# Attention block: row maxima split on GpSimd, turned by VectorE and carried through DRAM; row-sum copy in two parts; output weights rounded on GpSimd

## The chip, the cores and the metric

One core of one Trainium2 chip. Five engines run their own instruction queues: TensorE (PE, with its weight loads PEld), VectorE (DVE), ScalarE (ACT), GpSimd (POOL) and SyncE (SP), which issues most DMAs. The metric is the device time of one execution in microseconds (us), as the median of several runs.

## The reference

One transformer block on 2048 tokens of width 640, in float32:

```python
qkv = layernorm(x) @ wqkv                     # 32 heads of 20
scores = einsum("bhqd,bhkd->bhqk", q, k) * 20 ** -0.5
h = x + reshape(einsum("bhqk,bhkd->bhqd", softmax(scores), v)) @ wo
out = h + (silu(z @ w_gate) * (z @ w_up)) @ w_down   # z = layernorm(h), F = 1728
```

## The kernel before, in words

Three stages follow one another. First come layernorm and the qkv projection, whose results go to DRAM. Then the attention, from about 323 to 1475 us of the span. Then the output projection and the feed-forward part.

**Units and steps.** The attention is cut into 32 units `u`: eight groups of four heads, times four chunks of 512 queries (`u % 4` is the chunk). A unit has 16 steps `kt`, one for each 128 keys. A step multiplies four heads' keys with the queries (`scores`, L1187: four matmuls, each into one of four PSUM banks that are used in turn, `ps_one`), ACT takes the exponential out of each bank (L1193, 128x512), and two steps later PE multiplies the values with the exponentials (`weigh`, L1197: eight matmul records, into the bank `acc`). These eight open each step in PE's order (`W` in the strings `ORDER`); in this text **W** is their start, and the distance from one W to the next is the length of a step.

**Row maxima.** The exponent needs each query's largest score beforehand. Its negative is carried as two extra rows of the query tile `q_stk` (a rounded high part and the rest), against rows of ones in the keys, so that the score matmul subtracts it (62 rows: 60 and these 2). The maxima of later units are computed in the steps of earlier ones: each step has three more matmuls into `ps_max` (three banks in turn, L244), and DVE reduces each to one column of `mx` (L250). A list `singles` hands them out in order; a unit's maxima end some steps before the unit starts: about 5 steps for `u % 4 == 3` and for unit 1, at least 10 for the rest.

**The end of a unit's maxima.** When its last one is out, `max_all` (L257) reduces `mx` on DVE to `neg`, 128 queries x 16. Two steps later, at the step's W, `max_finish` turns it: PE transposes it (L264) into one of the four `ps_one` banks, ACT rounds it out of the bank (L88, 16x128), DVE subtracts for the rest (L89), and SP issues four DMAs (L271) into the two rows of `q_stk`.

**Row sums.** After a unit's last step `row_sums` (L1207) copies `acc` to the tile `o` on ACT. The next unit's weighing goes to the same bank, so its first W waits for that copy. DMAs gather the row sums, DVE takes their reciprocals after step 4 (L1218), a DMA spreads them (`rb`), GpSimd multiplies at step 9 (L1232), and SP stores `o` at step 11 (L1235).

**GpSimd and SP beside it.** From unit 1 on each step but 3 and 4 also takes one task of `prepare_weights`: GpSimd splits feed-forward weights into high and low parts (L1005, L1006), which SP stores to DRAM one task later (L996). `split_wo` (L883) splits the five row blocks of `wo` in units 25 to 27, at steps 2 and 3: ACT rounds (L88), GpSimd subtracts (L89). Each engine works through its own queue in the order of the program text; an instruction that waits holds all that stand behind it on that engine.

Of the kernel before, what the change touches and what calls it, by code (L numbers as in the profile page):

```python
# [9 lines left out]
F32 = mybir.dt.float32  # L10
BF16 = mybir.dt.bfloat16
F32R = mybir.dt.float32r
I32 = mybir.dt.int32
AF = mybir.ActivationFunctionType
ALU = mybir.AluOpType
AX = mybir.AxisListType

P = 128
# [7 lines left out]
CH = 512  # L26
NC = S // CH
TPC = CH // P
NF = (F + P - 1) // P
G = 4  # L30
# [3 lines left out]
NPART = 3 * DH  # L34
ROW = P // 2
# [9 lines left out]
def tile_block(ctx: ExitStack, tc: tile.TileContext, x, wqkv, wo, wg, wu, wd, out):  # L45
    nc = tc.nc
    x = x[0]
    out = out[0]
# [7 lines left out]
    v_d = dram.tile([S, NG, VG], F32, name="v_d")  # L56
    o_d = dram.tile([D, S], F32, name="o_d")
    r_d = dram.tile([H, S], F32, name="r_d")
    z_d = [dram.tile([P, 2 * ND * CH], F32R, name=f"z_d{c}") for c in range(2)]
    t_d = [dram.tile([P, 8 * CH], F32R, name=f"t_d{i}") for i in range(2)]  # L60
    w_d = [dram.tile([P, 8, 4 * P], F32R, name=f"w_d{f}") for f in range(NF)]
# [25 lines left out]
    def split(src, hi, lo, lo_engine=nc.vector):  # L87
        nc.scalar.activation(hi, src, AF.Copy)  # L88
        lo_engine.tensor_tensor(out=lo, in0=src, in1=hi.bitcast(F32), op=ALU.subtract)  # L89
# [46 lines left out]
    keys, queries, values = {}, {}, {}  # L136
# [117 lines left out]
    def max_all(u):  # L254

        ends[u] = stk.tile([P, G * TPC], F32, name="neg", tag="neg", bufs=2)
        nc.vector.tensor_reduce(  # L257
            ends[u], mxs[u].rearrange("p b h t k -> p (b h t) k"), axis=AX.X, op=ALU.max, negate=True
        )

    def max_finish(u):

        m = (ps_one if u else ps_max)()[: G * TPC, :P]
        nc.tensor.transpose(m, ends.pop(u), ident)  # L264
        parts = stk.tile([G * TPC, 2, P], F32R, name="m2", tag="m2", bufs=1)
        split(m, parts[:, 0], parts[:, 1], nc.vector)
        for b in range(2):
            for i in range(2):
                row = b * ROW + NPART + i
                first = b * 2 * TPC  # L270
                nc.sync.dma_start(  # L271
                    queries[u][row : row + 1].bitcast(F32).rearrange(
                        "r j (t p) -> r (j t) p", t=TPC
                    ),
                    parts[first : first + 2 * TPC, i, :].bitcast(F32),
                )
# [604 lines left out]
        nc.sync.dma_start(wo_raw[k], wo[k * P : (k + 1) * P, :])  # L881

    def split_wo(k):  # L883
        split(wo_raw.pop(k), wo_hi[:, k, :], wo_lo[:, k, :], nc.gpsimd)

    def projection(c, ps_of):

# [315 lines left out]
            )  # L1203

    def row_sums(acc, *queues):
        o = pc.tile([P, CH], F32, name="o", bufs=1)
        nc.scalar.activation(o, acc, AF.Copy)  # L1207
        r = pc.tile([P, 16], F32, name="r")
        for j in range(G):
            queues[j % len(queues)].dma_start(  # L1210
                r[32 * j : 32 * j + 32, :],
                o[32 * j + DH : 32 * j + DH + 1, :].rearrange("r (p f) -> r p f", p=32),
            )
        return o, r
# [21 lines left out]
                o_d[h * DH : (h + 1) * DH, c * CH : (c + 1) * CH], o[32 * j : 32 * j + DH, :]  # L1236
            )

    todo, tail, accs, closing, now = [], [], {}, {}, [0]
    singles = [[(*a, b) for a in rest] for b in range(2)]  # L1240
    left = {u: sum(2 for a in rest if a[0] == u) for u in range(1, NU)}

    def next_max(b):
        if singles[b]:
            a = singles[b].pop(0)
            max_one(*a)
            left[a[0]] -= 1
            if left[a[0]] == 0:
                max_all(a[0])
                closing[a[0]] = now[0] + 2  # L1250

    def weigh_next():
        u, kt, probs = todo.pop(0)
# [9 lines left out]
    for u in range(NU):  # L1263
        g, c = divmod(u, NC)
        if g == NG - 1 and c >= 2:
            _, first, ln, flips, _ = ahead
            extra = [*first, *ln, lambda: None, *flips]
        for kt in range(NT):
            now[0] = u * NT + kt
            ready = [v for v, at in closing.items() if at == now[0]]  # L1270
            probs = [pp.tile([P, 2, CH], F32, name="probs") for _ in range(2)]
            heads = [[0, 2], [1, 3]]
            order = ORDER[now[0] % 2] if singles[0] or singles[1] else "sSsSW"
            for op in order:
                if op in "mM":
                    next_max(int(op == "M"))
                elif op in "sS":
                    scores(u, kt, heads[op == "S"].pop(0), probs)
                else:
                    if len(todo) == 2:  # L1280
                        weigh_next()
                    for v in ready:
                        max_finish(v)
                    if extra:
                        extra.pop(0)()
                    if preparing and u and kt not in (3, 4):
                        preparing.pop(0)()
                    if now[0] == (NU - NC) * NT + 8:
                        unit_ring, last_ring = weight_rings()
                        unit_ring.fill()  # L1290
                        last_ring.fill()
            todo.append((u, kt, probs))
            if kt == 6 and u + 3 < NU:
                load_queries(u + 3)
            if kt == 10 and u == 0:
                fill_ones(k_stk[1])
            if kt >= 8 and kt % 2 == 0 and c == 1 and g + 1 < NG:
                load_keys(g + 1, slice((kt - 8) // 2 * CH, (kt - 6) // 2 * CH))
            if kt >= 8 and kt % 2 == 0 and c == 2 and g + 1 < NG:
                load_values(g + 1, (kt - 8) // 2 * TPC, (kt - 6) // 2 * TPC)  # L1300

            sooner = u >= NU - 2
            if kt == (3 if sooner else 4) and tail:
                reciprocals(u - 1, tail[0][2], nc.sync)
                rb = spread(u - 1, nc.sync)
            if kt == (6 if sooner else 9) and tail:
                store_o(u - 1, tail[0][1], rb, nc.gpsimd, None)
            if kt == (7 if sooner else 11) and tail:
                store_o(u - 1, tail.pop()[1], rb, None, nc.sync)
            if g == NG - 1 and c >= 1:  # L1310
                at = 8 if sooner else NT - 4
                if kt == at:
                    ahead = projection(
                        c - 1, ps_max if c < NC - 1 else (lambda: ps_b())
                    )
                if kt in (at, at + 1, 12 if sooner else 14):
                    ahead[0][min(kt - at, 2)]()
                    if kt == at + 1 and c < NC - 1:
                        ahead[4]()
            k = 2 * (u - NU + 8)  # L1320
            if kt in (12, 13) and 0 <= k + kt - 12 < ND:
                if k + kt == 12:
                    assert not preparing
                    wo_hi = pc.tile([P, ND, D], F32R, name="wo_hi", bufs=1)
                    wo_lo = pc.tile([P, ND, D], F32R, name="wo_lo", bufs=1)
                load_wo(k + kt - 12)
            if kt in (2, 3) and 0 <= k + kt - 4 < ND:
                split_wo(k + kt - 4)
# [566 lines left out]
```

## Time and profile before

| what | value |
|---|---|
| median of three runs | 2043.51 us (2040.27 to 2043.73) |
| profiled execution, its own time | 2038.82 us |
| its span, first to last instruction | 2037.0 us |
| mean granted TensorE clock | 0.999 |
| span of the attention stage with row maxima | about 323 to 1400 us |
| HBM traffic over the span | 151 GB/s |

A group row names the line, engine, operation, output and inputs, shape and count, then the busy time in us and the mean of one in ns, then the idle time of the engine before these instructions and who ended it. A row of the timeline has the start in us, the length in us, engine, line, operation, tiles, shape and how many instructions were merged into it; in brackets stands the idle time before it and what ended it. A row of stages has the stretch, its length, and each engine's busy time.

### The profile page before, as it was taken

What the parts mean: (1) busy time and instruction counts of PE and PEld (TensorE: products, weight loads), DVE (VectorE), ACT (ScalarE), POOL (GpSimd) and SP (SyncE); (2) the same over time, 40 slices, a digit from 0 to 9 for tenths busy, and PEclk for the clock granted to TensorE, in tenths of its full rate; (3) what the DMA queues carried; (4) which work ended last, traced back from release to release, by engine and by line L of the source; (5) the groups of instructions that cost most, each with busy time, mean ns of one, the idle gap of its engine ahead of it and who ended that gap; (6) DMA issues with size and microseconds to landing.
All of it is one profiled execution on the core that took longest, in us unless ns stands there. A gap on an engine that the chain in (4) does not pass through costs nothing.

```text
span 2037.0 us, 40049 instructions
## 1 busy us (share of the span) xinstructions
PE 2012.7 (99%) x14322; PEld 1249.9 (61%) x14322; DVE 1607.9 (79%) x2826; ACT 1445.2 (71%) x2855; POOL 774.1 (38%) x1103
## 2 busy tenths in 40 slices
PE   8999999999999999999999999999999999999999
PEld 6989995343334333334333433345598888888888
DVE  5677778888888888888888888886378666676677
ACT  4677778999999999999999999987633222211221
POOL 6464423334342444352400011011146454754555
PEclk9999999999999999999999999999999999999999
DMA  7877563452634534435512131311158654974542
GB/s 244 255 244 260 175 206 89 116 161 79 187 104 124 166 115 143 149 127 176 156 46 79 27 94 44 92 62 55 33 184 302 220 192 157 344 273 158 202 150 94
DMA packets 194062, 310.01 MB, mean 152 GB/s; under 512 B 47760, under 2 KB 82576, under 8 KB 192840
## 3 DMA queue, kind: packets, MB, share of 16 engines
q1 hardware_dynamic: 187272, 283.85, 43.0%
q0 software_dynamic: 6496, 23.60, 4.0%
q8 instruction: 114, 1.87, 0.4%
q14 instruction: 84, 0.69, 0.1%
q10 hardware_dynamic: 96, 0.00, 0.0%
HBM read 207.75 MB, written 98.83 MB: 151 GB/s over the span
## 4 chain that ended last, share of the span: by engine, by line
PE 87%; DMA 3%; DVE 1%; issue 1%; POOL 1%; ACT 1%; SPq 1%; ACTq 0%; DVEq 0%; POOLq 0%
PE acc L1197 24%; PE ps_one L1187 16%; PE ps_a L1358 15%; PE ps_max L244 12%; PE ps_b L1452 8%; PE ps_one L568 6%; PE ps_max L211 2%; PE ps_max L918 2%; PE ps_b L918 1%; DMA units<-w_d 1%; DMA halves<-j_d 0%; DMA h<-in_A_x 0%; PE ps_max L953 0%; DVE tmp L1573 0%; ACT o L1207 0%
## 5 line engine op out<-in xcount | busy, mean ns | idle before, releaser
L1193 ACT ACTIVATE probs<-ps_one 128x512 f32<-128x512 f32 x2048 | 1056.7, 614 | 62.3 <-PE ps_one L1187 37.6
L250 DVE TENSOR_REDUCE mx<-ps_max 128x1 f32<-128x512 f32 x1472 | 926.2, 684 | 106.9 <-PE ps_one L1187 75.6
L1187 PE MATMUL ps_one<-q_stk,k_stk 62*128 62x512 f32 x2048 | 586.0, 450 | 2.8 <-DVE m L89 1.8
L1197 PE MATMUL acc<-probs,v_stk 128*32 128x512 f32 x4096 | 545.2, 604 | 0.0
L1187 PEld LDWEIGHTS ps_one<-q_stk,k_stk 62*128 62x128 f32 x2048 | 251.5, 184 | 432.7 <-ACT probs L1193 398.3
L244 PE MATMUL ps_max<-k_stk,q_stk 60*128 60x512 f32 x1472 | 381.2, 425 | 0.0
L244 PEld LDWEIGHTS ps_max<-k_stk,q_stk 60*128 60x128 f32 x1472 | 271.6, 186 | 24.1 <-DVE mx L250 0.9
L1573 DVE TENSOR_TENSOR tmp<-ps_a,tmp 128x512 f32<-128x512 f32 x208 | 141.2, 689 | 120.3 <-PE ps_a L1358 94.6
L233 DVE TENSOR_REDUCE mx<-ps_max 128x2 f32<-128x512 f32 x288 | 180.6, 685 | 66.5 <-PE ps_max L211 63.4
L1232 POOL TENSOR_TENSOR o<-o,rb 128x512 f32<-128x512 f32 x31 | 39.9, 1287 | 413.3 <-DMA q_stk<-q_d 241.5
L1197 PEld LDWEIGHTS acc<-probs,v_stk 128*32 128x32 f32 x4096 | 80.6, 108 | 174.8 <-issue 166.2
L223 ACT ACTIVATE ps_max<-ps_max 128x512 f32<-128x512 f32 x288 | 151.7, 583 | 47.5 <-PE ps_max L211 44.7
L1452 PE MATMUL ps_b<-halves,yp 128*128 128x320 f32 x1032 | 179.3, 308 | 2.0 <-DMA halves<-j_d 1.2
L1452 PEld LDWEIGHTS ps_b<-halves,yp 128*128 128x128 f32 x1032 | 165.1, 188 | 18.6 <-POOL yp L89 1.5
L1358 PE MATMUL ps_a<-t,units 128*128 128x512 f32 x624 | 162.6, 396 | 0.0
L1358 PE MATMUL ps_a<-z,units 128*128 128x512 f32 x516 | 133.9, 394 | 0.0
L89 POOL TENSOR_TENSOR yp<-y,yp 128x256 fp32r<-128x256 f32 x96 | 60.4, 629 | 188.2 <-ACT yp L88 188.2
L1358 PEld LDWEIGHTS ps_a<-t,units 128*128 128x128 f32 x624 | 112.6, 188 | 18.9 <-ACT tmp L1586 0.3
L1457 DVE TENSOR_TENSOR h<-ps_b,h 128x320 f32<-128x320 f32 x248 | 110.0, 481 | 6.9 <-PE ps_b L1452 5.4
L568 PE MATMUL ps_one<-z_hi,w_lo 64*128 64x512 f32 x380 | 113.7, 395 | 0.0
L568 PE MATMUL ps_one<-z_hi,w_hi 64*128 64x512 f32 x380 | 113.1, 396 | 0.0
L568 PE MATMUL ps_one<-z_lo,w_hi 64*128 64x512 f32 x380 | 111.7, 393 | 0.0
(211 smaller groups left out, 2643.3 us busy)
## 6 DMA issues: line engine op xcount, KB each, us to landing
units<-w_d SPq DMA_DIRECT2D x186, 256.0 KB
w_d<-stage SPq DMA_DIRECT2D x106, 256.0 KB
halves<-j_d SPq DMA_DIRECT2D x70, 320.0 KB
j_d<-stage SPq DMA_DIRECT2D x42, 320.0 KB
k_stk<-k_d SPq DMA_DIRECT2D x64, 160.0 KB
q_stk<-q_d SPq DMA_DIRECT2D x64, 160.0 KB
raw<-k_d SPq DMA_DIRECT2D x62, 160.0 KB
raw<-q_d SPq DMA_DIRECT2D x54, 160.0 KB
```

Source lines behind the costliest of these rows:

```text
L223: nc.scalar.activation(ps, ps, AF.Relu)
L233: nc.vector.tensor_reduce(mx[:, b, :, t, kc], ps.rearrange("p (j n) -> p j n", j=2), axis=AX.X, op=ALU.max,)
L244: nc.tensor.matmul(ps, queries[u][rows, pair, t * P : (t + 1) * P], keys[u // NC][rows, pair, kc * CH : (kc + 1) * CH], start=True, stop=True,
L250: nc.vector.tensor_reduce(mxs[u][:, b, pair, t, kc : kc + 1], ps, axis=AX.X, op=ALU.max)
L568: nc.tensor.matmul(ps, a[rows], b[rows], start=(i == n == 0), stop=(i == 1 and n == last), skip_group_check=True,)
L1187: nc.tensor.matmul(ps, keys[u // NC][rows, p, kt * P : (kt + 1) * P], queries[u][rows, p, :], start=True, stop=True,)
L1193: nc.scalar.activation(probs[p][:, b, :], ps, AF.Exp, scale=scale)
L1197: nc.tensor.matmul(acc[32 * j : 32 * j + 32, :], values[u // NC][:, kt, j * VW : j * VW + 32], probs[j // 2][:, j % 2, :], start=(kt == 0) ...
L1358: nc.tensor.matmul(ps.rearrange("p (t n) -> p t n", t=TPC), w[k][:, i], z[k][:, :, j], start=(first and m == 0), stop=(last and m == len(n ...
L1452: nc.tensor.matmul(ps, a, b, start=(n == 0), stop=(n == len(pairs) - 1))
L1457: nc.vector.tensor_tensor(out=h, in0=ps, in1=h, op=ALU.add)
L1573: add = lambda out, ps, x: nc.vector.tensor_tensor(out=out, in0=ps, in1=x, op=ALU.add)
```

## The change

1. **Which units.** Units with `u % 4 == 3` and unit 1 keep `max_finish`. The other 22 (2, 4, 5, 6, 8, 9, 10, ... 28, 29, 30) go another way, in three pieces.
2. **`max_parts`** at the end of the step: GpSimd rounds `neg` and subtracts for the rest, both into one tile of 128x32.
3. **`max_turn`** four steps later: DVE turns that tile in blocks of 32x32, and SP writes it to DRAM (`m_d`, two tensors in turn).
4. **`max_load`** six steps after the end: SP loads it in four DMAs of 32 pieces of 128 bytes into the two rows of `q_stk`.
5. `max_all` is issued after all of the step's maxima, not right behind the unit's last one. `later` replaces `closing`.
6. **Row sums:** ACT copies 384 of `acc`'s 512 columns, DVE the other 128; `o` has two buffers.
7. **`split_wo`:** GpSimd does the rounding too.

```diff
-        split(wo_raw.pop(k), wo_hi[:, k, :], wo_lo[:, k, :], nc.gpsimd)
+        raw = wo_raw.pop(k)
+        nc.gpsimd.tensor_copy(wo_hi[:, k, :], raw)
+        nc.gpsimd.tensor_tensor(
+            out=wo_lo[:, k, :], in0=raw, in1=wo_hi[:, k, :].bitcast(F32), op=ALU.subtract
+        )
...
+    def max_parts(u):
+        neg = ends[u]
+        both = ends[u] = stk.tile([P, 2, G * TPC], F32R, name="neg2", bufs=2)
+        nc.gpsimd.tensor_copy(both[:, 0], neg)
+        nc.gpsimd.tensor_tensor(
+            out=both[:, 1], in0=neg, in1=both[:, 0].bitcast(F32), op=ALU.subtract
+        )
+    def max_turn(u):
+        turned = stk.tile([P, 2 * G * TPC], F32, name="turned", bufs=2)
+        nc.vector.transpose(turned, ends.pop(u).bitcast(F32).rearrange("p i n -> p (i n)"))
+        nc.sync.dma_start(m_d[u % 2], turned)
+    def max_load(u):
+        n = 2 * TPC
+        rows = m_d[u % 2].rearrange("(q i r) c -> i r q c", q=4, i=2)
+        for b in range(2):
+            for i in range(2):
+                row = b * ROW + NPART + i
+                dst = queries[u][row : row + 1].bitcast(F32).rearrange("r j c -> r (j c)")
+                nc.sync.dma_start(dst, rows[i, b * n : (b + 1) * n])
...
     def row_sums(acc, *queues):
-        o = pc.tile([P, CH], F32, name="o", bufs=1)
-        nc.scalar.activation(o, acc, AF.Copy)
+        o = pc.tile([P, CH], F32, name="o", bufs=2)
+        most = 3 * P
+        nc.scalar.activation(o[:, :most], acc[:, :most], AF.Copy)
+        nc.vector.tensor_copy(o[:, most:], acc[:, most:])
...
             if left[a[0]] == 0:
-                max_all(a[0])
-                closing[a[0]] = now[0] + 2
+                full.append(a[0])
...
-                    for v in ready:
-                        max_finish(v)
+                    for f in later.pop(now[0], ()):
+                        f()
...
             todo.append((u, kt, probs))
+            for v in full:
+                max_all(v)
+                if v % NC == NC - 1 or v == 1:
+                    later.setdefault(now[0] + 2, []).append(lambda v=v: max_finish(v))
+                else:
+                    max_parts(v)
+                    later.setdefault(now[0] + 4, []).append(lambda v=v: max_turn(v))
+                    later.setdefault(now[0] + 6, []).append(lambda v=v: max_load(v))
+            full.clear()
```

Three places show the order that results. On PE, at the start of unit 8, where unit 9's maxima are turned, before (`acc` is the weighing, `ps_one` are scores, `ps_max` maxima, `neg` the maxima to turn):

```order
L1197 MATMUL acc<-probs,v_stk_5591 32x512 x4
L264 MATMUL ps_one<-ident,neg 16x128
L1187 MATMUL ps_one<-q_stk,k_stk_123 128x512 x2
L244 MATMUL ps_max<-k_stk_123,q_stk 128x512 x2
L1187 MATMUL ps_one<-q_stk,k_stk_123 128x512 x2
```

and now:

```order
L1227 MATMUL acc<-probs,v_stk_5593 32x512 x4
L1217 MATMUL ps_one<-q_stk,k_stk_125 128x512 x2
L245 MATMUL ps_max<-k_stk_125,q_stk 128x512 x2
L1217 MATMUL ps_one<-q_stk,k_stk_125 128x512 x2
```

The transpose is gone from PE, and with it one turn of the four banks. On DVE at the same place, before (`mx` are the maxima, `neg` is `max_all`, `m` the subtraction of `max_finish`, `r` the reciprocals):

```order
L257 TENSOR_REDUCE neg<-mx_134 128x16
L250 TENSOR_REDUCE mx_135<-ps_max 128x1 x3
L89 TENSOR_TENSOR m_9646<-ps_one,m_9646 16x128
L250 TENSOR_REDUCE mx_135<-ps_max 128x1 x12
L1218 RECIPROCAL r<-r 128x16
```

and now:

```order
L258 TENSOR_REDUCE neg<-mx_136 128x16
L251 TENSOR_REDUCE mx_137<-ps_max 128x1 x3
L1239 COPY o<-acc 128x128
L251 TENSOR_REDUCE mx_137<-ps_max 128x1 x6
L274 STREAM_TRANSPOSE turned<-neg_9613 128x32
L251 TENSOR_REDUCE mx_137<-ps_max 128x1 x6
L1250 RECIPROCAL r<-r 128x16
```

The subtraction has left this queue; the copy of a quarter of `acc` stands in its place, where in the built program it waits for ACT's copy, and the turn follows two steps later. On SP, in unit 3 (`m_d` is the new DRAM tensor, `w_d` stores of split weights, `raw` loads of weights to split):

```order
L1026 DMA w_d_82<-stage 128x512 x2
L275 DMA m_d_70<-turned 128x32
L1026 DMA w_d_82<-stage 128x512
L1055 DMA raw<-in_B_w_gate 128x5x128
L1055 DMA raw<-in_B_w_up 128x5x128
L285 DMA q_stk<-m_d_70 1x32x32 x4
L1267 DMA o_d<-o 20x512 x4
```

The store stands at step 9 and the four loads at step 11, ahead of the store of `o`; the four DMAs that stood at step 7 are gone.

More of the change, by code (lines that the diff above doesn't have):

```diff
@@ L58, in tile_block @@
     r_d = dram.tile([H, S], F32, name="r_d")
+    m_d = [dram.tile([P, 2 * G * TPC], F32, name=f"m_d{i}") for i in range(2)]
     z_d = [dram.tile([P, 2 * ND * CH], F32R, name=f"z_d{c}") for c in range(2)]
@@ L1237, in store_o @@
             )
-    todo, tail, accs, closing, now = [], [], {}, {}, [0]
+    todo, tail, accs, later, full, now = [], [], {}, {}, [], [0]
     singles = [[(*a, b) for a in rest] for b in range(2)]
@@ L1269, in tile_block @@
             now[0] = u * NT + kt
-            ready = [v for v, at in closing.items() if at == now[0]]
             probs = [pp.tile([P, 2, CH], F32, name="probs") for _ in range(2)]
```

## The prediction

> **What bounds the kernel now.** I read the page's busy shares first, then the stages, then PE's timeline step by step.
>
> ```profile
> PE 2012.7 (99%) x14322; PEld 1249.9 (61%) x14322; DVE 1607.9 (79%) x2826; ACT 1445.2 (71%) x2855; POOL 774.1 (38%) x1103
> ...
> 323.00:1400.00 1077.00, 1074.25 (x7472) 435.20 (x7469) 947.53 (x1578) 1028.76 (x2025) 307.32 (x469) 1.00 0.36 110
> 1475.00:2037.00 562.00, 554.74 (x2927) 486.13 (x2925) 398.08 (x764) 131.41 (x274) 297.97 (x411) 1.00 0.60 207
> ```
>
> PE is busy nearly all the time, in the attention (1074.25 of 1077 us) and behind it (554.74 of 562). But a busy PE is no PE at its peak, since its matmuls overlap. What counts in the attention is the distance from one W to the next. ACT with 1028.76 us and DVE with 947.53 us have little room beside it, and GpSimd (307.32) has much. Here is PE's timeline of unit 9, the weighing alone, from step 2 to step 9, and under it the start of unit 8, steps 1 to 3.
>
> ```profile
> 638.05 1.06 PE L1197 MATMUL acc<-probs,v_stk 128*32 128x512 f32 x8
> 640.34 1.06 PE L1197 MATMUL acc<-probs,v_stk 128*32 128x512 f32 x8
> 642.46 1.06 PE L1197 MATMUL acc<-probs,v_stk 128*32 128x512 f32 x8
> 644.58 1.06 PE L1197 MATMUL acc<-probs,v_stk 128*32 128x512 f32 x8
> 646.69 1.06 PE L1197 MATMUL acc<-probs,v_stk 128*32 128x512 f32 x8
> 648.96 1.06 PE L1197 MATMUL acc<-probs,v_stk 128*32 128x512 f32 x8
> 651.33 1.07 PE L1197 MATMUL acc<-probs,v_stk 128*32 128x512 f32 x8
> 653.45 1.06 PE L1197 MATMUL acc<-probs,v_stk 128*32 128x512 f32 x8
> ```
>
> ```profile
> 601.32 1.06 PE L1197 MATMUL acc<-probs,v_stk 128*32 128x512 f32 x8
> 604.17 1.06 PE L1197 MATMUL acc<-probs,v_stk 128*32 128x512 f32 x8
> 606.30 1.06 PE L1197 MATMUL acc<-probs,v_stk 128*32 128x512 f32 x8
> ```
>
> A plain step takes 2.12 us (642.46 to 644.58). Three are longer in unit 9: 2.29 behind the copy of `acc` (638.05 to 640.34), then 2.27 and 2.37 (646.69 to 651.33). At the start of unit 8 the copy and a turn of maxima fall into one step: 2.85. All excess over 2.12 has a cause that can be named, and the change works on those causes. The timeline of all engines over the two long steps of unit 9 names them.
>
> ```profile
> 646.03 0.24 DVE L1218 RECIPROCAL r<-r 128x16 f32<-128x16 f32 x1
> 646.34 0.69 DVE L250 TENSOR_REDUCE mx<-ps_max 128x1 f32<-128x512 f32 x1
> 647.06 0.22 DVE L257 TENSOR_REDUCE neg<-mx 128x16 f32<-128x64 f32 x1
> ...
> 649.96 0.28 PE L264 MATMUL ps_one<-ident,neg 128*16 128x128 f32 x1
> 650.27 0.27 ACT L88 ACTIVATE m<-ps_one 16x128 fp32r<-16x128 f32 x1
> 650.57 0.28 DVE L89 TENSOR_TENSOR m<-ps_one,m 16x128 fp32r<-16x128 f32 x1 [0.23 <-ACT m L88]
> ...
> 650.90 0.18 PEld L1187 LDWEIGHTS ps_one<-q_stk,k_stk 62*128 62x128 f32 x1 [0.21 <-DVE m L89]
> ```
>
> The 2.37 is `max_finish`: a transpose of 0.28 on PE, ACT's 0.27 between two exponentials, DVE's 0.28, and a score that waits for the bank until 650.90. The 2.27 is DVE alone: the reciprocal at 646.03 fills DVE's gap of that step, and `max_all` one maximum later finds none, so the maxima run late and a `ps_max` bank comes free late.
>
> **The change part by part. Maxima that go the new way.** Unit by unit, the 22 turns fall into two kinds. Fifteen (`v % 4` of 0 or 2) stand at step 7 as in unit 9: 2.27 + 2.37 - 2 x 2.12 = 0.40 us each, 6.0 us. Seven (5, 9, ... 29) stand at step 1 as in unit 8: 2.85 - 2.13, less what the copy of `acc` costs alone (2.29 - 2.12), is 0.55 each, 3.9 us. I count all of it as gone, also the 0.15 of `max_all`: it moves behind the three maxima, to where DVE has its gap. If it stays dear, 15 x 0.15 = 2.2 us come back.
>
> What is added lies on DVE, GpSimd and SP. DVE's turn of 128x32 is not in the trace; the nearest row is the reciprocal of 128x16, 0.24 us. That one alone costs a step nothing (644.58 to 646.69 is 2.11), and the turn stands at steps 9 or 3, with no other extra next to it; so I take zero, and as upper end the 0.15 of the `max_all` case for 22 turns, 3.3 us. If its gap is filled, the maxima queued behind it are late, and W with them. GpSimd's two operations on 128x16 are hidden by its idle time; an instruction waits there for `max_all`, and weight tasks queue behind it, but at step 5 GpSimd is ahead of the program. DVE's turn has four steps, 8.5 us, before it would wait for them.
>
> ```profile
> L1232 POOL TENSOR_TENSOR o<-o,rb 128x512 f32<-128x512 f32 x31 | 39.9, 1287 | 413.3 <-DMA q_stk<-q_d 241.5 <-ACT probs L1193 97.3 <-DMA q_stk<-m 39.7
> ```
>
> GpSimd idles 413.3 us ahead of 31 multiplications, which is where it waits for the program.
>
> **wo on GpSimd.** ACT's five roundings lengthen the steps of units 25 to 27. PE's timeline of unit 25, W of steps 3 and 8:
>
> ```profile
> 1193.23 1.06 PE L1197 MATMUL acc<-probs,v_stk 128*32 128x512 f32 x8
> ...
> 1204.91 1.06 PE L1197 MATMUL acc<-probs,v_stk 128*32 128x512 f32 x8
> ```
>
> These five steps take 11.68 us, in unit 9 10.99 (640.34 to 651.33): 0.35 for each of two, 1.7 us for five. GpSimd has no weight tasks left there; the rounding of 640 columns is near its two larger casts:
>
> ```profile
> L1005 POOL CAST stage<-raw 128x320 fp32r<-128x320 f32 x30 | 13.6, 453 | 17.2 <-DMA raw<-in_B_w_down 17.2
> L521 POOL CAST z_hi<-e 128x512 fp32r<-128x512 f32 x8 | 4.9, 610 | 12.5 <-ACT e L510 12.5
> ```
>
> so about 0.7 us, three units ahead of use: free.
>
> **The copy of `acc` in two.** This is the doubtful part. ACT, DVE and PEld around the copy at the start of unit 11:
>
> ```profile
> 704.46 1.89 DVE L250 TENSOR_REDUCE mx<-ps_max 128x1 f32<-128x512 f32 x3 [0.25 <-PE ps_one L1187]
> 706.15 0.63 ACT L1207 ACTIVATE o<-acc 128x512 f32<-128x512 f32 x1
> 706.58 1.89 DVE L250 TENSOR_REDUCE mx<-ps_max 128x1 f32<-128x512 f32 x3 [0.24 <-PE ps_max L244]
> 706.93 0.16 PEld L1197 LDWEIGHTS acc<-probs,v_stk 128*32 128x32 f32 x8 [0.35 <-ACT o L1207]
> ```
>
> and two groups of nearby shapes:
>
> ```profile
> L707 ACT ACTIVATE ev<-ps_one 128x320 f32<-128x320 f32 x32 | 14.3, 446 | 1.7 <-PE ps_one L568 1.4
> L89 DVE TENSOR_TENSOR kept<-ps_a,kept 128x128 fp32r<-128x128 f32 x8 | 2.3, 283 | 1.0 <-ACT kept L88 0.9
> ```
>
> ACT's 320 columns take 0.45, its 512 take 0.63: 128 fewer save 0.12, so its copy ends at 706.66 instead of 706.78. In the built program DVE's part waits for ACT's. By the nearest row, 0.28 for 128x128 out of PSUM, it ends near 706.97. Behind it on DVE stand the three maxima, 0.3 later than their 706.58; and W at 706.93 waits for it, about 0.08. The late maxima then cost what `max_all` does, 0.15 at most, partly behind that wait. Against this, the exponentials come 0.12 earlier and today's 0.17 (2.29 - 2.12) should go. I take +0.05 a unit, 1.5 us over 29 units. The ends: 0.17 gained and nothing lost, -4.9 us; both delays full and ACT's stall unchanged, +0.2 a unit, +5.8 us.
>
> Here a page bears on the sum. The Trainium skill, "PSUM — Partial Sum Buffer", section "PSUM bank collisions raise a hardware error", says that two engines must not touch the same bank and partitions at once, reads of ScalarE and VectorE included. That speaks against the split: the two parts run one after the other, as the built program has them. By a rule without it they would run side by side and the sum would be at the lower end above; no row of before shows such a pair.
>
> **The plain step.** It is not one length: W of unit 13, steps 9 to 12, are 2.13 apart.
>
> ```profile
> 793.86 1.06 PE L1197 MATMUL acc<-probs,v_stk 128*32 128x512 f32 x8
> ...
> 800.25 1.07 PE L1197 MATMUL acc<-probs,v_stk 128*32 128x512 f32 x8
> ```
>
> (800.25 - 793.86) / 3 = 2.13, against 2.12 in unit 9. Each turn shifts which of the four banks a score gets, and fewer turns will mix these states anew: 0.007 either way over 450 steps is 3 us, with no sign known. I take zero.
>
> **Sum.** -6.0 - 3.9 - 1.7 + 1.5 = -10.1 us. The stages behind the attention start that much earlier; PE, busy for 554.74 of 562 us there, sets their length as before. The profiled execution took 2038.82 us, its span 2037.0 and 1.8 around it: 2028.7. The median shown, 2043.51, stands 4.7 above that execution; the same 10.1 taken from it gives **2033.4 us**.
>
> **Rivals.** (1) DVE becomes the bound: split copy, turn and `max_all` each push the maxima. For it: 1.89 us of reductions in a step of 2.12, and the 2.27 above. Against it: the gap takes one extra of 0.24 without loss. With +0.2 a unit (5.8 instead of 1.5) and `max_all`'s 2.2 back, -10.1 + 4.3 + 2.2 gives 2039.9. (2) The copy is clean, -4.9 instead of +1.5: 2027.0. (3) The turns cost nothing now, because PE waits for ACT in each step anyway and a shorter step only waits longer; then only wo's 1.7 and the copy's 1.5 are left: 2043.3. Against it stands that the excess sits in single steps and that the plain ones between do not give it back. (4) The other side: rows that arrive late. From `max_load` to use are five steps. PE needs unit 6's rows at its first score, SP is loaded in unit 5:
>
> ```profile
> 519.65 1.06 PE L1197 MATMUL acc<-probs,v_stk 128*32 128x512 f32 x8
> ...
> 531.31 0.50 PE L1187 MATMUL ps_one<-q_stk,k_stk 62*128 62x512 f32 x2
> ```
>
> ```profile
> 508.20 0.60 SPq L1220 DMA_DIRECT2D r_d<-r  x1
> 510.19 0.57 SPq L1226 DMA_DIRECT2D rb<-r_d  x1
> ...
> 513.52 5.34 SPq L271 DMA_DIRECT2D q_stk<-m  x4
> ...
> 526.92 2.98 SPq L1235 DMA_DIRECT2D o_d<-o  x4
> ```
>
> Step 11 has its W at 519.65, and SP issues that step's stores only at 526.92. Four loads there, some 3 us of issue and 2 us to land (508.20 to 510.19, a store and the wait for it), end at 531.9, 0.6 us past the need. It decides from 7 us of lag on SP; 2 us late at 15 units is 30 - 10.1 = +20, 2063. Against it: the 5.34 us at 513.52 leave this place, and the loads stand ahead of those stores. The Trainium skill, "DMA: Bandwidth & Descriptors", section "Specifications", has transfers below 512 B as read-modify-write; the new pieces have 128. By it landing would be longer and this rival likelier; the row above, in pieces of 64 B, needed 2 us at most, so the trace gives it little.
>
> **Chances.** Forecast (2029 to 2038) 0.58, rival 1 0.14, rival 2 0.10, rival 3 0.10, rival 4 0.08. About 0.2%, 4 us, is what a measurement of this kernel can tell from no change: faster is below 2039.4. Rival 1 lies on that line; I give 0.10 of it to faster. Faster 0.78, same 0.14, slower 0.08. Range: down to 2026 for a clean copy, up to 2041 for rival 1 with part of the 3 us of the plain step; rivals 3 and 4 stay outside.
>
> **What would show it.** Right: no long step at step 7 where the turn is gone; the first step of units 8, 12, ... at 2.3 instead of 2.85; DVE's copy starting when ACT's ends; wo's steps plain. Wrong: W behind the copy over 2.4, a wait of DVE for GpSimd at the turn, or a wait of a unit's first scores for a DMA.

## The result and the profile after

The changed kernel took 2030.46 us (median of 5 runs, 2030.02 to 2035.07), the kernel before 2043.51 (2040.27 to 2045.22) beside it: ratio 0.9951, 95% interval 0.9940 to 0.9961. The forecast was 2033.4, with a range of 2026 to 2041 and faster at 0.78. The profiled execution took 2030.02 us, its span 2028.2 (before 2038.82 and 2037.0), at the same granted clock of 0.999. One execution of a later run, late_load, took 2711.6 us at a granted clock of 0.654 and is left out of its median below.

The page's busy times, and the row of stages for the attention (the stretch ends 10 us earlier than the one shown of before):

```profile
PE 2003.0 (99%) x14300; PEld 1249.2 (62%) x14300; DVE 1610.5 (79%) x2858; ACT 1436.5 (71%) x2828; POOL 785.9 (39%) x1152
...
323.00:1390.00 1067.00, 1065.04 (x7451) 434.57 (x7449) 949.50 (x1606) 1019.77 (x1997) 320.00 (x519) 1.00 0.37 111
```

PE is as busy as before (1065.04 of 1067). In the attention ACT is 9 us less busy, DVE 2 us more, GpSimd 13 us more. Busy shares tell no more than that; the distances of W do. Here PE's timeline of unit 9, W of steps 6 to 8, and the start of unit 8, W of steps 1 to 3, places that the prediction shows of before:

```profile
645.13 1.06 PE L1227 MATMUL acc<-probs,v_stk 128*32 128x512 f32 x8
647.25 1.06 PE L1227 MATMUL acc<-probs,v_stk 128*32 128x512 f32 x8
649.36 1.06 PE L1227 MATMUL acc<-probs,v_stk 128*32 128x512 f32 x8
...
600.13 1.07 PE L1227 MATMUL acc<-probs,v_stk 128*32 128x512 f32 x8
602.37 1.07 PE L1227 MATMUL acc<-probs,v_stk 128*32 128x512 f32 x8
604.58 1.07 PE L1227 MATMUL acc<-probs,v_stk 128*32 128x512 f32 x8
```

The two long steps of unit 9 are gone: steps 6 and 7 take 2.12 and 2.11 where 2.27 and 2.37 stood. The start of unit 8 has 2.24 and 2.21 where 2.85 stood; what is left there is the copy of `acc`. So each named excess of before can be compared with what is left of it.

To add them up over the whole attention, this text takes the distance from the first W of unit 1 to the first W of unit 30, 29 units of 16 steps. Of before:

```profile
357.47 1.07 PE L1197 MATMUL acc<-probs,v_stk 128*32 128x512 f32 x8
...
1361.36 1.06 PE L1197 MATMUL acc<-probs,v_stk 128*32 128x512 f32 x8
```

and of after:

```profile
357.92 1.06 PE L1227 MATMUL acc<-probs,v_stk 128*32 128x512 f32 x8
...
1351.89 1.07 PE L1227 MATMUL acc<-probs,v_stk 128*32 128x512 f32 x8
```

That is 1003.89 against 993.96 us: **-9.93**, where the prediction has -10.1. The span fell by 8.8; the other 1.1 us lie ahead of unit 1 (0.45) and behind unit 30 (0.7), in stages that the change does not touch. In the runs below these stretches vary by more: the first W of unit 1 stands between 357.36 and 361.32. Measured against each unit's own median step, and summed over the 29 units, the excess is:

| steps of a unit | what lies there | before | after |
|---|---|---|---|
| 0 to 2 | copy of `acc`, before also 7 turns | 8.39 us | 5.69 us |
| 6 and 7 | 15 turns with their `max_all` | 5.55 | -0.04 |
| 4 and 5 of units 25 to 27 | rounding of `wo` | 1.79 | -0.01 |
| 12 | the 7 turns that are kept | 1.79 | 1.76 |
| sum | | 17.52 | 7.40 |

The sum falls by 10.1, and the plain steps take 0.2 of it back. Nothing of this size is left without a name.

The new operations themselves, from the groups by tile of the changed kernel (minimum, median and maximum in ns), with the one wait that GpSimd's rounding has:

```profile
L274 DVE STREAM_TRANSPOSE turned<-neg x22: 199/201/203, 378.8 to 1338.4; 128x32 f32<-128x32 f32 x22
L266 POOL CAST neg<-neg x22: 193/196/198, 372.7 to 1332.3; 128x16 fp32r<-128x16 f32 x22
L267 POOL TENSOR_TENSOR neg<-neg,neg x22: 220/221/223, 372.9 to 1332.6; 128x16 fp32r<-128x16 f32 x22
...
  DVE neg L258: 256.2, 20
```

DVE's turn takes 0.20 us and no engine is named as waiting for it. GpSimd waits for DVE (256 us in 20 times), which it can afford, and DVE never waits for GpSimd.

### The profile page after: what moved, and what is told of

It is laid out like the page before. It is cut to its first block, busy times and chain, and to the rows that moved or that the text cites. A ratio compares the mean times of both kernels' runs of the same rounds, so it can differ in the third digit from the quotient of the medians.

```text
span 2028.2 us, 40006 instructions
## 1 busy us (share of the span) xinstructions
PE 2003.0 (99%) x14300; PEld 1249.2 (62%) x14300; DVE 1610.5 (79%) x2858; ACT 1436.5 (71%) x2828; POOL 785.9 (39%) x1152
## 4 chain that ended last, share of the span: by engine, by line
PE 89%; DVE 1%; DMA 1%; issue 1%; ACT 1%; SPq 0%; POOL 0%; DVEq 0%; ACTq 0%; POOLq 0%
PE acc L1227 25%; PE ps_a L1397 15%; PE ps_one L1217 15%; PE ps_max L245 13%; PE ps_b L1491 8%; PE ps_one L594 6%; PE ps_max L212 2%; PE ps_max L948 2%; PE ps_b L948 2%; DMA halves<-j_d 1%; ACT probs L1223 0%; PE ps_max L983 0%; DVE tmp L1612 0%; SPq L1173 0%; SPq L297 0%
## 5 line engine op out<-in xcount | busy, mean ns | idle before, releaser
L1217 PE MATMUL ps_one<-q_stk,k_stk 62*128 62x512 f32 x2048 | 577.9, 447 | 1.0 <-ACT probs L1223 0.8
L245 PE MATMUL ps_max<-k_stk,q_stk 60*128 60x512 f32 x1472 | 371.6, 425 | 0.0
```

Source lines behind the costliest of these rows:

```text
L245: nc.tensor.matmul(ps, queries[u][rows, pair, t * P : (t + 1) * P], keys[u // NC][rows, pair, kc * CH : (kc + 1) * CH], start=True, stop=True,
L1217: nc.tensor.matmul(ps, keys[u // NC][rows, p, kt * P : (kt + 1) * P], queries[u][rows, p, :], start=True, stop=True,)
```

## The experiments

Theory: the excess of single steps was the whole gain, by the terms of the prediction's sum, and the copy in two gives a little back. Rivals: the steps around the copy lose more (or gain) than 0.05 a unit; PE waits for ACT in any case, so that removed excess buys nothing; the rows in `q_stk` arrive late. Distances below are those of the profiled execution, from W of unit 1 to W of unit 30; the kernel before has 1003.89, the changed one 993.96. The ratios are to the kernel before.

| run | median us | ratio, 95% interval | distance |
|---|---|---|---|
| turns_alone | 2035.91 | 0.9966 (0.9955 to 0.9977) | 995.80 |
| copy_alone | 2040.89 | 1.0000 (0.9991 to 1.0010) | 1004.75 |
| wo_alone | 2038.20 | 0.9988 (0.9978 to 0.9997) | 1002.30 |
| max_all_moved | 2039.31 | 0.9993 (0.9983 to 1.0002) | 1002.91 |
| whole_copy | 2031.50 | 0.9946 (0.9929 to 0.9963) | 992.14 |
| half_copy | 2032.46 | 0.9950 (0.9935 to 0.9965) | 995.19 |
| one_buffer | 2032.28 | 0.9953 (0.9937 to 0.9969) | 994.36 |
| late_load | 2078.04 | 1.0177 (1.0160 to 1.0194) | 1039.21 |
| early_load | 2033.11 | 0.9954 (0.9940 to 0.9968) | 993.72 |
| whole_early | 2029.68 | 0.9939 (0.9925 to 0.9954) | 992.09 |
| whole_all | 2054.01 | 1.0057 (1.0044 to 1.0071) | 1014.23 |

**turns_alone**: only the new way of the 22 turns. In the changed kernel:

```diff
-        o = pc.tile([P, CH], F32, name="o", bufs=2)
-        most = 3 * P
-        nc.scalar.activation(o[:, :most], acc[:, :most], AF.Copy)
-        nc.vector.tensor_copy(o[:, most:], acc[:, most:])
+        o = pc.tile([P, CH], F32, name="o", bufs=1)
+        nc.scalar.activation(o, acc, AF.Copy)
...
-        raw = wo_raw.pop(k)
-        nc.gpsimd.tensor_copy(wo_hi[:, k, :], raw)
-        nc.gpsimd.tensor_tensor(
-            out=wo_lo[:, k, :], in0=raw, in1=wo_hi[:, k, :].bitcast(F32), op=ALU.subtract
-        )
+        split(wo_raw.pop(k), wo_hi[:, k, :], wo_lo[:, k, :], nc.gpsimd)
```

> The 22 maxima go the new way and max_all stands behind the step's maxima; the copy of the sums and the split of wo are as before. Theory (the excess sits in single steps and goes with PE's transpose): 6.0 + 3.9 = 9.9 us less than before, span near 2027; the step behind the copy stays at 2.29 us, steps 7 are plain. Rival 'PE waits for ACT anyway': within 1 us of before. Rival 'DVE is the bound': the turn of 0.20 us lengthens its step by up to 0.15, and the gain is 6.6 us.

Measured: -8.1 in the distance. Steps 6 and 7 fall from 5.55 to -0.01, as in the changed kernel, and the joint steps of 2.85 are gone. 1.7 us are lost to single waits: the first steps of units 10 and 18 are 0.3 and 0.4 too long (rows that arrive late, see early_load and late_load), and at the start of unit 6 two steps take 3.06 and 2.39. The timeline of this kernel at that place, SP with it:

```profile
533.10 1.60 SPq L1261 DMA_DIRECT2D o_d<-o  x4
...
537.09 0.60 ACT L1233 ACTIVATE o<-acc 128x512 f32<-128x512 f32 x1 [0.95 <-DMA k_stk<-k_d]
537.74 0.16 PEld L1223 LDWEIGHTS acc<-probs,v_stk 128*32 128x32 f32 x8 [1.30 <-ACT o L1233]
```

The copy writes the only buffer of `o`, whose stores SP had issued at 533.10 to 534.70, late; ACT waits 0.95 for a DMA, and W 1.30 for ACT. The profile names a load of keys as that DMA, which the copy does not read; that it is the stores of `o` is argued from the one buffer. Without the waits the turns are worth -9.8, against -9.9 predicted. The rival that PE waits for ACT anyway (2043.3, turns worth nothing) is out.

**copy_alone**: only the copy in two with its two buffers, in the kernel before (the four lines of `row_sums` in the diff of the change).

> Only the copy of the sums is in two parts. Theory (DVE's part runs behind ACT's and holds W and the maxima): two steps of about 2.22 in place of one of 2.29 and one of 2.12, +0.04 us a unit, +1.3 us in all. Rival 'the two parts run side by side and the stall goes': -0.17 a unit, -4.9 us. Rival 'DVE is the bound': +0.2 a unit, +5.8 us.

Measured: +0.86, ratio 1.0000. The excess of steps 0 to 2 rises from 8.39 to 9.49, +1.10, of which 1.03 lie in the 22 units whose copy stands alone: 0.05 each. In the 7 joint starts the step stays at 2.85 to 2.87 but for one of 2.95, so that the copy costs next to nothing there. Both the clean copy (-4.9) and DVE as the bound (+5.8) are excluded; the interval of the ratio, +-2 us, holds neither.

**wo_alone**: only the rounding of `wo` on GpSimd, in the kernel before (the first hunk of the diff of the change).

> Only the rounding of wo has moved to GpSimd. Theory: the long steps 4 and 5 of units 25 to 27 (2.41 and 2.65) become plain, -1.7 us. Rival 'something else is late there': those steps stay above 2.3 and less than 0.5 us is gained.

Measured: -1.59. Steps 4 and 5 of units 25 to 27 fall from 1.79 to -0.03. GpSimd's rounding hides as thought.

**max_all_moved**: only the place of `max_all`, behind all of the step's maxima, in the kernel before; `max_finish` stays for all units.

```diff
-                max_all(a[0])
-                closing[a[0]] = now[0] + 2
+                full.append(a[0])
...
             todo.append((u, kt, probs))
+            for v in full:
+                max_all(v)
+                closing[v] = now[0] + 2
+            full.clear()
```

> Only max_all has moved behind the three maxima of its step; PE still turns every unit's maxima. Theory (with the reciprocal just ahead of it max_all found no gap on DVE): step 6 of odd units falls from 2.27 to 2.12, 15 x 0.15 = -2.2 us, and step 7 stays at 2.37. Rival 'both long steps belong to the transpose': step 6 stays at 2.27 and the time within 0.5 us of before.

Measured: -0.98 in all, instead of -2.2. PE's timeline in unit 9, W of steps 6 to 8:

```profile
647.87 1.06 PE L1197 MATMUL acc<-probs,v_stk 128*32 128x512 f32 x8
649.98 1.06 PE L1197 MATMUL acc<-probs,v_stk 128*32 128x512 f32 x8
652.36 1.07 PE L1197 MATMUL acc<-probs,v_stk 128*32 128x512 f32 x8
```

Step 6 is plain now (647.87 to 649.98, before 2.27), step 7 keeps its 2.38. Steps 6 and 7 together fall from 5.55 to 3.72: -1.83 for 15 turns, 0.12 each. So a `max_all` that follows the reciprocal and stands ahead of a maximum costs 0.12 a time, and behind the maxima it costs nothing. About 0.6 come back in units 4 and 6; in unit 6 the copy of `acc` starts 0.35 late.

**whole_copy**: the changed kernel with the copy whole on ACT, the two buffers kept.

```diff
-        most = 3 * P
-        nc.scalar.activation(o[:, :most], acc[:, :most], AF.Copy)
-        nc.vector.tensor_copy(o[:, most:], acc[:, most:])
+        nc.scalar.activation(o, acc, AF.Copy)
```

> The changed kernel, but ACT copies all 512 columns of the sums again, into two buffers as the change has them. Theory (the split copy costs 0.045 us a unit net): the two steps of 2.23 and 2.22 at a unit's start become one of about 2.28, and the distance from unit 1 to unit 30 is 1.3 us shorter than in the changed kernel. Rival 'the split helps because ACT is short of time': about 3 us longer.

Measured: -1.83 against the changed kernel, and that with a first step of 2.73 in unit 18, where rows came late. The times of the two can't be told apart (0.9946 and 0.9951). whole_early below repeats it without that wait.

**half_copy**: the changed kernel with half of `acc` on each engine.

```diff
-        most = 3 * P
+        most = 2 * P
```

> The changed kernel, but ACT copies 256 columns of the sums and DVE, behind it, the other 256. Theory (W waits for DVE's part, which starts when ACT's ends): DVE's part takes 0.42 instead of 0.29 and ACT's saves 0.11, so W behind the copy is only 0.02 later, but the three maxima run 0.13 later: both steps together 0.05 to 0.15 longer, +1.5 to +4.5 us over 29 units. Rival 'the two run side by side': no change or shorter.

Measured: the two steps take about 2.24 and 2.23 at the start of unit 11, against 2.23 and 2.22; +0.03 a unit on the mean, less than the 0.05 expected at least. The distance is 1.23 longer: 0.87 in steps 0 to 2, of which 0.1 is a late first step of unit 10, and the rest in plain steps. This timeline shows why half is hardly dearer than a quarter:

```profile
704.20 1.06 PE L1227 MATMUL acc<-probs,v_stk 128*32 128x512 f32 x8
705.51 0.42 ACT L1238 ACTIVATE o<-acc 128x256 f32<-128x256 f32 x1
705.77 3.78 ACT L1223 ACTIVATE probs<-ps_one 128x512 f32<-128x512 f32 x7
705.96 0.42 DVE L1239 COPY o<-acc 128x256 f32<-128x256 f32 x1 [0.25 <-ACT o L1238]
706.30 3.20 DVE L251 TENSOR_REDUCE mx<-ps_max 128x1 f32<-128x512 f32 x5
706.44 1.06 PE L1227 MATMUL acc<-probs,v_stk 128*32 128x512 f32 x8
```

0.42 and 0.42 one behind the other end at 706.38, 0.87 after the start; the quarter's 0.53 and 0.29 (the changed kernel's rows follow under the third point of the next section) end 0.85 after theirs. What ACT saves DVE adds.

**one_buffer**: the changed kernel with one buffer for `o`.

```diff
-        o = pc.tile([P, CH], F32, name="o", bufs=2)
+        o = pc.tile([P, CH], F32, name="o", bufs=1)
```

> The changed kernel, but with one buffer for the copy of the sums. Theory (the loads now stand ahead of the stores of the sums on SP, which in units 5 and 9 go out at the very end of the unit): the copy waits for those stores at the start of units 6 and 10, 1 to 2 us in each, nothing elsewhere; +2 to +3 us. Rival 'the second buffer does nothing': no difference in any step.

Measured: +0.4, no wait at unit 6 (2.22 and 2.21) and none elsewhere that the copy names. So the waits that I expected at units 6 and 10 did not come in this execution. The wait exists (0.95 us in turns_alone, 0.17 in wo_alone, both with one buffer), but whether it comes depends on how late SP is; what the second buffer is worth on the mean stays open.

**late_load**: the changed kernel with the four loads four steps later, to price rows that arrive late.

```diff
-                    later.setdefault(now[0] + 6, []).append(lambda v=v: max_load(v))
+                    later.setdefault(now[0] + 10, []).append(lambda v=v: max_load(v))
```

> The changed kernel, but the four loads of the turned rows stand ten steps behind the end of the maxima instead of six. Theory of late rows: in the 15 units with v % 4 of 0 or 2 the loads then stand one step ahead of use; 2.6 us of issue and 2 us to land against 3.1 us: PE waits 1.5 us in each, 22 us, and more in units 6, 10, 14, 18, where SP is behind. Rival 'the rows land in well under 2 us or PE makes up for it': under 8 us.

Measured: +45.2, about twice what was expected, and in 7 units only (2, 6, 10, 12, 14, 18, 26). PE's waits, in total, times and longest, and then the timeline at the start of unit 10 with SP:

```profile
PE ps_one L1217 <- DMA q_stk<-m_d: 30.9, 8, 6.0
```

```profile
683.34 2.12 SPq L152 DMA_DIRECT2D k_stk<-k_d  x4
685.83 2.79 SPq L285 DMA_DIRECT2D q_stk<-m_d  x4
...
689.94 1.15 PE L1217 MATMUL ps_one<-q_stk,k_stk 62*128 62x512 f32 x2 [5.94 <-DMA q_stk<-m_d]
691.91 1.93 PE L1227 MATMUL acc<-probs,v_stk 128*32 128x512 f32 x8
```

The loads stand behind eight key loads and stores that SP works off late; the scores wait 5.94. Then come the eight weighing records of W, which take 1.93 together instead of 1.07. The row of stages says why; the last three figures of a row are the granted clock, the DMA share and GB/s:

```profile
690.50:694.00 3.50, 3.50 (x17) 1.13 (x18) 1.89 (x3) 2.11 (x5) 0.00 (x0) 0.50 0.14 53
694.00:697.50 3.50, 3.50 (x21) 1.72 (x22) 2.18 (x4) 2.70 (x6) 0.00 (x0) 0.74 0.02 2
```

After the idle time PE runs at half the clock; the 0.74 says that this lasts through about half of the second row, to 695.8, which is 5.9 us after PE went on. Over all seven units, in stretches of 1 us, the clock stood at 0.50 for 6.8 us in five of them and for 3.4 us in two (14 and 26). The Trainium skill, "TensorE: Matmul & The Clock Gate", section "What's actually happening", has TensorE fall to half rate after an idle window of about 3.4 us and come back after about 3.4 busy ones. The size agrees, 3.4 us or twice that. But in units 14 and 26 the clock fell behind waits of 2.9 and 3.0 us, and in unit 10 it took 5.9 us to come back; the measurement decides. So 30.9 us of waiting became 45.2: a late row costs its wait, and about half as much again for the clock.

**early_load**: the changed kernel with turn and loads one and two steps earlier.

```diff
-                    later.setdefault(now[0] + 4, []).append(lambda v=v: max_turn(v))
-                    later.setdefault(now[0] + 6, []).append(lambda v=v: max_load(v))
+                    later.setdefault(now[0] + 3, []).append(lambda v=v: max_turn(v))
+                    later.setdefault(now[0] + 4, []).append(lambda v=v: max_load(v))
```

> The changed kernel with the turn three steps and the loads four steps behind the parts (instead of four and six): one thing changed, the rows' margin. Theory (rival 4 is real but just missed: in the changed kernel the rows of one unit, 10, came 0.2 us late because SP issued its loads some 9 us behind the program): no unit's first step is longer than 2.15 us, the distance of W from unit 1 to unit 30 is 0.2 us shorter than the changed kernel's 993.96, and the time the same within 1 us. Rival (the first step of unit 10 has another cause than late loads): it stays at 2.3 us or more. A second way to be wrong: the turn one step earlier waits for GpSimd or falls in a step without a gap, and step 6 or 8 becomes longer by 0.1 us or more in 22 units, +2 us.

First the changed kernel at this place: the loads for unit 10 on SP, W of step 11 of unit 9 and of step 0 of unit 10, and the weights of a score of unit 10 that waits.

```profile
655.72 1.06 PE L1227 MATMUL acc<-probs,v_stk 128*32 128x512 f32 x8
...
658.22 3.95 SPq L152 DMA_DIRECT2D k_stk<-k_d  x4
663.51 2.80 SPq L285 DMA_DIRECT2D q_stk<-m_d  x4
...
666.30 1.07 PE L1227 MATMUL acc<-probs,v_stk 128*32 128x512 f32 x8
...
667.71 0.18 PEld L1217 LDWEIGHTS ps_one<-q_stk,k_stk 62*128 62x128 f32 x1 [0.23 <-issue]
```

The loads belong to step 11 (655.72) and went out at 663.51, 7.8 us behind; the score waited 0.23, for which the profile names nothing ("issue"), and the step from 666.30 on took 2.33. And early_load, the loads and the first two scores, merged into one row without a wait between them (the 0.84 ahead of them is the wait for ACT that each step has):

```profile
661.85 2.77 SPq L285 DMA_DIRECT2D q_stk<-m_d  x4
...
668.26 0.19 PEld L1217 LDWEIGHTS ps_one<-q_stk,k_stk 62*128 62x128 f32 x2 [0.84 <-ACT probs L1223]
```

Measured: the first step of unit 10 is plain (2.12), and so is that of each other unit; steps 6 to 8 are not longer. Late loads were the cause. The distance is 0.25 shorter, as expected, but not for the reason given: in the changed kernel the late step of unit 10 took the place of the copy's excess (its next steps are 2.13 and 2.14), so that the wait itself cost nothing on balance. The 0.25 lies in the plain steps.

**whole_early**: early_load with the whole copy of whole_copy.

> The changed kernel with the early loads of early_load and the copy of acc whole on ACT in two buffers. Theory: the split costs 0.04 us a unit (a step of 2.23 and one of 2.22 instead of one of 2.27), and in the whole copy's run before this one 0.8 us were lost to late rows in units 10 and 18; without them the distance of W from unit 1 to unit 30 is 991.3 us (-2.6 against the changed kernel), the time about 2028 to 2030 us. Rival (the split costs nothing by itself and the shorter distance came from plain steps of 2.117 instead of 2.130, which fall as they like): 993 to 994 us.

Measured: 992.09, -1.63 against early_load, between the two expectations. The excess of steps 0 to 2 is 4.46 against early_load's 5.78: -1.32, 0.046 for each of 29 units; the rest of the 1.63 lies in plain steps. It has the lowest time of all (2029.68, profiled 2028.12), but its interval overlaps with that of the changed kernel.

**whole_all**: whole_early with the seven kept turns on the new way too, turn and loads one step behind the parts. The edit moves the turn of unit 31 too, which lies behind the first W of unit 30 and so outside the distance.

```diff
-                if v % NC == NC - 1 or v == 1:
+                if v == 1:
...
+                    soon = v % NC == NC - 1
-                    later.setdefault(now[0] + 3, []).append(lambda v=v: max_turn(v))
-                    later.setdefault(now[0] + 4, []).append(lambda v=v: max_load(v))
+                    later.setdefault(now[0] + (1 if soon else 3), []).append(lambda v=v: max_turn(v))
+                    later.setdefault(now[0] + (1 if soon else 4), []).append(lambda v=v: max_load(v))
```

> As whole_early, and the seven kept turns of units 3, 7, ... 27 go the new way too, with the turn and the loads one step behind the parts. Theory (each kept turn costs the 0.25 us of its step of 2.38 and nothing else): 2 us less than whole_early, 989.5 us from unit 1 to unit 30. Rival (rows that arrive late): for these units the loads stand at step 12, one step later than the changed kernel's at step 11, and SP's lag of up to 9 us makes the next unit's first scores wait; at 2 us each that is +14 us, about 1005. DVE may also wait for GpSimd at these turns, 0.4 us or more each, +3.

Measured: +22.1 against whole_early, and neither for the gain nor for the rows: the units after the seven start with plain steps. DVE's waits say where it went (total, times, longest), and the timeline of GpSimd in unit 10, with DVE's turn, how:

```profile
DVE turned L274 <- POOL neg L267: 17.3, 7, 6.2
```

```profile
696.86 0.72 POOL L1067 TENSOR_TENSOR sums<-raw 128x256 f32<-128x256 f32 x1 [20.09 <-DMA raw<-in_B_w_up]
...
700.24 0.73 POOL L1072 TENSOR_TENSOR sums<-raw,sums 128x256 f32<-128x256 f32 x1
700.91 0.20 POOL L266 CAST neg<-neg 128x16 fp32r<-128x16 f32 x1
701.19 0.22 POOL L267 TENSOR_TENSOR neg<-neg,neg 128x16 fp32r<-128x16 f32 x1
701.45 0.21 DVE L274 STREAM_TRANSPOSE turned<-neg 128x32 f32<-128x32 f32 x1 [6.19 <-POOL neg L267]
```

GpSimd had itself waited 20 us, until 696.86, for a load of weights that SP issued only at 687.69, and five operations (the first and the last are shown) stood ahead of the rounding. DVE waited 6.19 for it, the maxima behind the turn with it, and then PE, whose granted clock fell to 0.50 as in late_load (702.0 to 705.9): one step of 8.6 and one of 3.7 in unit 10. Units 14 and 18 went the same way, with waits of DVE of 4.02 and 4.66. In the other four units DVE waited only some 0.6, and the step grew from 2.38 to about 2.74. The wait of DVE was among the rivals, at +3 us; what it cost was some seven times that. The kept turns are kept where the new way has no slack.

## Why the prediction was right

1. **Turns at step 7:** -6.0 predicted, -5.59 measured (0.37 instead of 0.40 each). `max_all`'s part is 0.12, not 0.15; max_all_moved shows that the new place alone takes it away.
2. **Turns at step 1:** -3.9 predicted. Without the split copy, steps 0 to 2 fall from 8.39 to 4.46 (whole_early): -3.93.
3. **The copy:** +0.05 a unit predicted, +0.046 measured (early_load against whole_early), +0.05 in copy_alone. The changed kernel's timeline at the start of unit 6:

```profile
531.57 1.07 PE L1227 MATMUL acc<-probs,v_stk 128*32 128x512 f32 x8
532.89 0.53 ACT L1238 ACTIVATE o<-acc 128x384 f32<-128x384 f32 x1
533.26 4.13 ACT L1223 ACTIVATE probs<-ps_one 128x512 f32<-128x512 f32 x8
533.45 0.29 DVE L1239 COPY o<-acc 128x128 f32<-128x128 f32 x1 [0.36 <-ACT o L1238]
533.66 3.80 DVE L251 TENSOR_REDUCE mx<-ps_max 128x1 f32<-128x512 f32 x6
533.79 0.16 PEld L1227 LDWEIGHTS acc<-probs,v_stk 128*32 128x32 f32 x8 [0.47 <-DVE o L1239]
536.02 1.07 PE L1227 MATMUL acc<-probs,v_stk 128*32 128x512 f32 x8
```

   against whole_early at the start of unit 11:

```profile
702.22 0.16 PEld L1227 LDWEIGHTS acc<-probs,v_stk 128*32 128x32 f32 x8 [0.35 <-issue]
703.55 0.63 ACT L1237 ACTIVATE o<-acc 128x512 f32<-128x512 f32 x1
704.34 0.16 PEld L1227 LDWEIGHTS acc<-probs,v_stk 128*32 128x32 f32 x8 [0.36 <-ACT o L1237]
706.19 0.18 PEld L1217 LDWEIGHTS ps_one<-q_stk,k_stk 62*128 62x128 f32 x1 [0.31 <-ACT probs L1223]
706.62 0.16 PEld L1227 LDWEIGHTS acc<-probs,v_stk 128*32 128x32 f32 x8 [0.25 <-issue]
```

   Whole, the step up to the W that waits is plain (2.12) and the next one takes 2.28: a score waits 0.31 for the exponentials, which are late behind a copy of 0.63. In two, W comes 0.1 later (a step of 2.23 on the mean of the units), as DVE's part starts when ACT's ends; and that wait of the score is gone: from unit 1 to unit 30 PE's weight loads wait 457 times for exponentials in early_load and 486 times in whole_early, once more in each of the 29 units. Yet the next step is only 0.06 shorter (2.22 on the mean), so that some 0.09 of excess stay in it, for which the profile names no wait. half_copy bears on them: its exponentials start 0.67 us ahead of W (705.77 and 706.44) where the changed kernel has 0.53, its maxima about as far ahead (0.14 and 0.13), and this step is as long, 2.22. So what is left goes with DVE's late maxima rather than with ACT, as the prediction's sum has it; this is argued from the two runs, and none moves the maxima alone. The terms were 0.08 for the wait, up to 0.15 for the maxima and -0.17 for the exponentials; by this reading they came out at 0.10, 0.09 and -0.15.
4. **`wo`:** -1.7 predicted, -1.59 alone and -1.80 in the changed kernel.
5. **DVE's turn:** zero taken. No step of 2.12 became longer for it, at step 9 or one step earlier in early_load.
6. **Late rows:** the 7 us of lag from which they decide is about right. The changed kernel is at 7.8 in unit 10 and loses 0.2 in that step; it is the one unit of 22 there, though units 10 and 18 show up to 0.6 in other runs. By the traces of the changed kernel, turns_alone, whole_copy and half_copy a lag of 7.3 and 7.6 cost nothing, and 7.7 to 8.2 cost 0.2 to 0.6. The price was too low: I counted waits alone, and late_load shows the clock on top. That rival stayed out since SP is that late in few units, not because its price was small.
7. **The level:** the 4.7 us between the shown median and the profiled execution, which I carried over, was not there in the changed kernel (2030.46 and 2030.02). By the spans alone the kernel gained 8.8, by the medians 13; the ratio's 10.0 lies between. In the later runs the kernel before has medians of 2041.27, 2041.78 and 2041.63, so that part of the 13 is a high draw of 2043.51. The forecast of 2033.4 lies 2.9 above the measured median by this level: 4.3 too much, less the 1.3 by which the profiled execution missed its 2028.7.

The sum is nearer to the measured one than its terms are: these came out at -5.6, -3.9, -1.8 and +1.3, and the 0.4 that the turns at step 7 fall short is mostly made up by `wo` (0.1) and the copy (0.2). That the sum closes to 0.2 us is in part luck.

What the working left out is the second buffer of `o`: with one, the copy waited 0.95 us in one execution and not at all in another. The split copy by itself is a small loss; the gain of the change is all in the turns (with the new place of `max_all`) and in `wo`.

## What to carry to other kernels

Where one engine is busy for 99% of a stage, measure the length of its steps and give every step above the plain one a cause; the sum of those excesses forecast this change to 0.2 us, with errors of up to 0.4 in its terms. Work moved to an engine with much idle time needs slack counted in that engine's queue: GpSimd idles for most of the stage, and still an operation that DVE needed one step later came 6 us late behind a load. A copy that two engines share out of one bank ran as two copies in a row, and the wait for the second took more than the first had saved.

## What the runs showed of the hardware

- Waits of PE of 2.9 to 6.0 us, 30.9 in all, cost 45.2 (late_load): the granted clock stood at 0.50 for 3.4 or 6.8 us around the end of each, and a step at that clock took up to 3.86 us instead of 2.13 (3.87 in whole_all).
- Two engines' copies out of one bank, one right behind the other, hand over in about 0.03 us (ACT 532.89 + 0.53, DVE at 533.45).
- Copies out of PSUM to SBUF took on ACT 0.60 to 0.63, 0.53 and 0.42 us for 512, 384 and 256 columns, on DVE 0.42 and 0.29 for 256 and 128.
- DVE turned 128x32 in blocks in 0.20 us, less than the 0.24 of a reciprocal of half the size. GpSimd needed 0.20 and 0.22 us for a cast and a subtraction of 128x16.
